# Finer array tiles in the start-up, other banks for the second batch's keys, and a re-sorted instruction order in an attention-then-GLU kernel

## The chip, the cores and the metric

The kernel runs on one core of a Trainium2 chip. The time is the device time of that core in microseconds (us); the figure used is the median of the runs shown. Engines are named as the profile names them: PE is the matmul array (PEld its weight loads), DVE, ACT and POOL the three elementwise engines, SP the engine whose queue issues nearly all DMA transfers.

## The reference

A linear attention with second-order features, and a gated MLP on its output (4 batches, 4 heads, 1088 tokens, head size 32, 8+8 projections):

```python
def phi(x):
    a = np.einsum('rd,bhsd->bhsr', S1, x)
    b = np.einsum('rd,bhsd->bhsr', S2, x)
    return np.einsum('bhsi,bhsj->bhsij', a, b).reshape(*x.shape[:-1], r * r)
q_p, k_p = phi(q), phi(k)
kv = np.einsum('bhsf,bhsd->bhfd', k_p, v);  z = np.sum(k_p, axis=2)
out = einsum(q_p, kv) / (einsum(q_p, z) + 1e-06)          # per head
x = out as [4352 tokens, 128]
xn = x / sqrt(mean(x*x) + 1e-06) * rms_g
y = (silu(xn @ w_gate) * (xn @ w_val)) @ w_out            # d_ff = 1536
```

The weights arrive as 64-bit words and are turned into 32-bit floats on the chip.

## The kernel before

Tokens are cut into nine chunks c0 to c8 (eight of 512 columns, one of 256), and d_ff into twelve slices j. One pair of chunk and slice is a slot: three matmuls into `g_ps` (gate), three into `v_ps` (value), Silu on ACT to `s`, the product `h` on DVE, and the down projection into `o_ps`. Gate and value always take three passes (`x_hi`·`w_hi`, `x_hi`·`w_lo`, `x_lo`·`w_hi`). The down projection is one fp32 matmul (`o_ps<-h,w_f`) in the first twelve slots and the last ones; in all others `h` is split into `h_hi` (a cast, mostly ACT) and `h_lo` (a subtraction, on DVE or POOL) and three passes follow. Slots run c0 with j 0-5, c1 with j 0-5, c0 with j 6-11, c1 with j 6-11, then c2 to c8 whole.

Ahead of a chunk's slots stands its attention. For each batch the keys `kt` go through PE with the small projection `s_t` (lines 489), ACT brings half of the result to `ab`, an outer product makes the features `phi`, and PE sums `phi` against the values `vt` into kv. Batch 0 does this with `o_ps` as accumulator (lines 541); batches 1 to 3 take another form with 32 columns of the array per head (lines 410 to 440). Queries of c0 and c1 go the same way, in token order: A and B by PE (line 582), `abq` on ACT, the outer product `phn` on DVE, a transpose on PE (601), a copy `phiq`. From c2 on, A and B are made transposed (685), copied to `abt`, sent to DRAM (`far`) and read back spread over rows as `at` and `bt`, whose product is `phiq` (line 651, one instruction for each of two halves p0 and p1, on POOL or DVE). Then come the numerator and denominator (669), division, the root (POOL, `rstd`), the scaling `xn`, a transpose (772) and `x_hi`/`x_lo`.

Each weight slice takes an Abs (`w_tmp<-w_raw`, ACT or DVE), four DVE steps (318, 323, 328, 332; the last gives `w_f`), a cast `w_hi` on ACT and a subtraction `w_lo` on POOL.

The order is not that of the code. Every step is put into a `Plan` with a key (its urgency, in slots), a guessed duration on each engine that may do it, and sometimes a penalty for one of them. `Plan.run` places them one by one on guessed clocks and then writes the instructions out in order of guessed start. On the chip each engine works through its own list strictly in that order, so an instruction that waits holds up all that stand behind it in its list. In a wait early in the program the planner has PE do dummy matmuls (line 300).

[...]

Of the kernel before, what the change touches and what calls it, by code (L numbers as in the profile page):

```python
# [21 lines left out]
F = R * R  # L22
NT = B * S
P = 128
# [3 lines left out]
KT = 9  # L28
SP = KT * P
HALF = 64  # L30
# [28 lines left out]
HOP = 160  # L59
COPY_DVE = 600  # L60
REST_DVE = 500
ABS_ACT = -300
NATURAL = 2
PHIS = 2
PUT_DVE = 100
PHIQ_DVE = 600
CUT = 6
TURNED = (1, 2, 3)
HBUFS = 3
# [1 line left out]
EXACT = 2  # L71
EARLY = 12
SPLIT = 6
HEAD = 2
K1 = -41,9,10,-28.2
VT1 = (-15, -14, -13)
SBD = (1,)
AB2 = (-21, -20, -19)
KVO = ()
Q0 = (-61, -57, -56)  # L80
LATER = 12
KLATE = 2500
DLAT = 2400
CHAIN = -52
WAIT = 150
WKEY = {0: -50, 1: -43}
XN_ACT = 150
Q0L = -97.8
Q1 = (8, 6, 5)
Q1L = -25  # L90
KO = (20, 18, 16)
QO = (20, 10, 6)


# [116 lines left out]
def attention_then_glu(ctx, tc, kT, v, qT, sw, w, gain, out):  # L211
    nc = tc.nc
# [9 lines left out]
    def ps(name, bufs):  # L222
        return plan.buf(psum, [P, 512], F32, name, bufs)

    def pe(ns, key, emit, reads, writes, part=False):
        plan.add({"pe": (ns, emit, 0, part)}, key, reads, writes)
# [52 lines left out]
    for b in range(B):  # L279
        t = const.tile([P, 2, 2 * (D + 1)], F32, name=f"kv{b}")  # L280
# [6 lines left out]
    sblk_t = const.tile([P, NB], F32, name="s_t")  # L287
# [110 lines left out]
    abs_of, ahead = {}, {}  # L398
# [65 lines left out]
    def kside(b, keys, early):  # L464
        first = b == 0
        kab, kphi, key = keys
        kt, vt, kv = sb("kt", [P, SP], 2), sb("vt", [P, KT, H, VA], 2), kvs[b]
# [11 lines left out]
        piece = [next(g for g, (_, e) in enumerate(pieces) if hi <= e) for _, hi in groups]  # L479
        abs_ = [sb("ab", [P, 2, 3, H, R], 3) for _ in groups]  # L480
        phis = [sb("phi", [P, 3, H * F], 4) for _ in groups]
# [20 lines left out]
        for i, (lo, hi) in enumerate(groups):  # L502
            g, m, ts = piece[i], hi - lo, slice(0, hi - lo)
            ab_ps, o = (banks[i], 0) if first else (banks[i // 2], i % 2 * 3 * HALF)
            ab, phi = abs_[i], phis[i]
# [28 lines left out]
        acc = ps("o_ps", 1) if first or b in KVO else ps("att", 3)  # L534
        for i, (lo, hi) in enumerate(groups):
            def kvmm(lo=lo, hi=hi, phi=phis[i]):
                kvv = acc()[:, :2 * VA].rearrange("p (a x) -> p a x", x=VA)
                for t in range(lo, hi):
                    for h in range(H):
                        rows = slice((h % 2) * F, (h % 2 + 1) * F)  # L540
                        nc.tensor.matmul(
                            out=kvv[rows, h // 2, :], lhsT=phi()[:, t - lo, h * F:(h + 1) * F], rhs=vt()[:, t, h, :],
                            start=(t == 0 and h < 2), stop=(t == KT - 1), skip_group_check=True,
                        )

            pe(275 * (hi - lo), key, kvmm, [(phis[i], i), (vt, piece[i])], [acc], True)
        for hh in range(2):
            def put(eng, rows=slice(hh * F, (hh + 1) * F), xs=slice(hh * (D + 1), (hh + 1) * (D + 1))):
                kvv = acc()[:, :2 * VA].rearrange("p (a x) -> p a x", x=VA)
# [15 lines left out]
    def qphi(c, kab):  # L565
        n = CHUNKS[c]
        nt = n // P
        first = c == 0
        key0 = kab
        q, phi = phiqs[c]  # L570
        if c < NATURAL:

            ab, pn = sb("abq", [P, 4, H, R], 1), sb("phn", [P, 4, H * F], 1)
            for u in range(0, nt, 2):
                kab = key0 + (1 if first and u else 0)
                us = slice(u, u + 2)
                ab_ps = ps("att", 3)
                tr = ps(("g_ps", "v_ps")[u // 2], 2) if first else ps("att", 3)

                def abmm(u=u, ab_ps=ab_ps):  # L580
                    for t in range(2):
                        nc.tensor.matmul(
                            out=ab_ps()[:, t * HALF:(t + 1) * HALF], lhsT=q()[:, (u + t) * P:(u + t + 1) * P], rhs=sblk_t,
                            start=True, stop=True,
                        )

                def near(ab_ps=ab_ps):
                    return ab_ps()[:, :2 * HALF].rearrange("p (th c r) -> p th c r", c=2, r=R)

                def outer(us=us, near=near):  # L590
                    nc.vector.tensor_tensor(
                        out=pn()[:, us].rearrange("p t (h i j) -> p (t h) i j", h=H, i=R),
                        in0=near()[:, :, 0, :].unsqueeze(3).to_broadcast([P, 2 * H, R, R]),
                        in1=ab()[:, us].rearrange("p t h r -> p (t h) r").unsqueeze(2).to_broadcast([P, 2 * H, R, R]),
                        op=ALU.mult,
                    )

                def turn(u=u, tr=tr):
                    for p in range(2):
                        for t in range(2):  # L600
                            nc.tensor.transpose(
                                out=tr()[:, (2 * p + t) * P:(2 * p + t + 1) * P], in_=pn()[:, u + t, p * P:(p + 1) * P], identity=ident
                            )

                pe(440, kab, abmm, [q, "sblk"], [ab_ps])
                act(
                    HALF, kab, lambda us=us, near=near: nc.scalar.copy(
                        out=ab()[:, us].rearrange("p t h r -> p (t h) r"), in_=near()[:, :, 1, :]
                    ), [ab_ps], [(ab, u)],
                )  # L610
                dve(2 * 268, kab, outer, [(ab, u), ab_ps], [(pn, u)])
                pe(440, kab, turn, [(pn, u)], [tr])

                def put(eng, u=u, tr=tr):
                    eng(out=phi()[:, :, u * P:(u + 2) * P], in_=tr().rearrange("p (a s) -> p a s", a=2))

                plan.add({
                    "act": (512 * 0.835 + 144, lambda put=put: put(nc.scalar.copy), 0),
                    "dve": (512 * 1.04 + 140, lambda put=put: put(nc.vector.tensor_copy), PUT_DVE),
                }, kab, [tr], [(phi, u)])  # L620
        else:


            m = n // 2
            ab, at, bt = sb("abt", [P, 256], 2), sb("at", [P, 2, 512], 1), sb("bt", [P, 2, 512], 1)
            ab_ps = abs_of[c]
            act(m, kab, lambda: nc.scalar.copy(out=ab()[:, :m], in_=ab_ps()[:, :m]), [ab_ps], [ab])
            far = plan.buf(dram, [2 * H * R, 512], F32, "far", 2)
            for t in range(2):
                load(  # L630
                    H * R * n * 4, kab, lambda t=t: nc.sync.dma_start(
                        out=far()[:, t * m:(t + 1) * m], in_=ab()[t * HALF:(t + 1) * HALF, :m]
                    ), [(far, t)], [ab],
                )
            for p in range(2):
                rows = slice(2 * p * R, 2 * (p + 1) * R)
                load(
                    P * n * 8, kab, lambda p=p, rows=rows: nc.sync.dma_start(
                        out=at()[:, p, :n], in_=far()[rows, :n].unsqueeze(1).to_broadcast([2 * R, R, n])
                    ), [(at, p)], [(far, 0), (far, 1)],  # L640
                )
                for o in range(2):
                    rows = slice((H + 2 * p + o) * R, (H + 2 * p + o + 1) * R)
                    load(
                        F * n * 8, kab, lambda p=p, o=o, rows=rows: nc.sync.dma_start(  # L645
                            out=bt()[o * F:(o + 1) * F, p, :n], in_=far()[rows, :n].unsqueeze(0).to_broadcast([R, R, n])
                        ), [(bt, p, o)], [(far, 0), (far, 1)],
                    )

                def times(eng, p=p):  # L650
                    eng.tensor_tensor(out=phi()[:, p, :n], in0=at()[:, p, :n], in1=bt()[:, p, :n], op=ALU.mult)  # L651

                plan.add({
                    "pool": (n * 2.1 + 150, lambda times=times: times(nc.gpsimd), 0),
                    "dve": (n * 1.04 + 140, lambda times=times: times(nc.vector), PHIQ_DVE, True),
                }, kab, [(at, p), (bt, p, 0), (bt, p, 1)], [(phi, "p", p)])
# [35 lines left out]
    def qside(c, keys, also=None):  # L692
        n, s0 = CHUNKS[c], STARTS[c]
        nt = n // P
        first = c == 0
        phi = phiqs[c][1]
        x, xn = sb("x", [P, 4, DM], 2), sb("xn", [P, 4, DM], 1)
# [14 lines left out]
        for u in range(0, nt, 2):  # L712
# [17 lines left out]
            if first and not u:  # L730
                for t in range(2):
# [3 lines left out]
                            out=sq()[:, t], in0=x()[:, u + t], in1=x()[:, u + t], scale=1.0 / DM, scalar=EPS,  # L735
# [4 lines left out]
            if c < ACCUM:  # L740
                for t in range(2):
# [3 lines left out]
                            out=sq()[:, t], in_=x()[:, u + t], func=AF.Square, accum_out=ss()[:, u + t:u + t + 1]  # L745
# [9 lines left out]
        for u, wd in ((0, 2), (2, 2)) if first else ((0, nt),):  # L755
# [2 lines left out]
            xt = ps("att", 3)  # L758
            if first and not u:

                ahead[1] = [ps("att", 3) for _ in range(2)]
            ids = list(range(u, u + wd, 2))

            def root(us=us):
# [14 lines left out]
            if u or not first:  # L779
                dve(  # L780
                    5, kturn, lambda us=us: nc.vector.tensor_scalar(  # L781
                        out=ms()[:, us], in0=ss()[:, us], scalar1=1.0 / DM, scalar2=EPS, op0=ALU.mult, op1=ALU.add
# [130 lines left out]
    for t, (c, j) in enumerate(slots):  # L913
        slot(c, j, t)
        if j == (CUT - 1 if c == 0 else NJ - 1):
            if c + 2 < len(CHUNKS):
                t2 = begin[c + 2]
                if c == 0:
                    qload(2, AB2[0])
                    job = abmm(2)  # L920
# [60 lines left out]
```

## Time and profile before

| | |
|---|---|
| median of 3 runs | 266.39 us (266.28 to 266.45) |
| the profiled execution: its time / its span | 267.68 us / 265.9 us |
| PE busy, DVE, ACT, POOL | 260.0, 189.6, 153.0, 66.8 us |
| granted PE clock | 1.000 |
| DMA, mean over the span | 83 GB/s |

The span runs from the first to the last instruction; the time also holds what lies around them. In the rows, `x24` counts records: an fp32 matmul leaves two, so 36 matmuls are 72 records. The duration of a matmul record contains some 0.2 us of latency; the pace of a row of them is read from start to start.

### The profile page before, as it was taken

The numbers are of one execution on the slowest core, as the hardware profiler recorded it, in microseconds if no ns is written. First come the engines' busy times: TensorE is split into PE (matmuls) and PEld (weight loads), VectorE is DVE, ScalarE is ACT, GpSimd is POOL, SyncE is SP. The second block draws the span as 40 slices with busy tenths as digits, with TensorE's granted clock in tenths as the row PEclk, the third lists the DMA queues.
The fourth block names the chain that finished last, engine by engine and source line by source line (L and its number), as shares of the span: only waits on it lengthen the run. The fifth ranks groups of instructions, "written<-read, shape, count | busy, mean of one in ns | idle before, by whom it ended". The sixth has DMA issues, their size and how long they took to land.

```text
span 265.9 us, 5111 instructions
## 1 busy us (share of the span) xinstructions
PE 260.0 (98%) x1913; PEld 206.8 (78%) x1913; DVE 189.6 (71%) x375; ACT 153.0 (58%) x319; POOL 66.8 (25%) x83
## 2 busy tenths in 40 slices
PE   8989999999989999999999999999999999999995
PEld 6877676678867887878887877788878888788894
DVE  3789997787956886677566796677667566766532
ACT  4377673484744644565556554665656565665662
POOL 5053661265060150002700220012200700100262
PEclk9999999999999999999999999999999999999999
DMA  6999801721511430035002500034002100100010
GB/s 201 362 382 313 264 2 32 218 64 62 148 49 53 125 85 2 1 101 145 13 2 79 140 20 4 0 101 118 1 0 76 55 0 0 42 1 0 0 42 21
DMA packets 13097, 22.11 MB, mean 83 GB/s; under 512 B 1680, under 2 KB 5904, under 8 KB 13072
## 3 DMA queue, kind: packets, MB, share of 16 engines
q1 hardware_dynamic: 12928, 21.72, 26.4%
q8 instruction: 15, 0.25, 0.4%
q14 instruction: 10, 0.08, 0.1%
q10 hardware_dynamic: 144, 0.07, 0.1%
HBM read 18.69 MB, written 3.08 MB: 82 GB/s over the span
## 4 chain that ended last, share of the span: by engine, by line
PE 84%; DMA 8%; SPq 3%; POOL 1%; ACT 1%; issue 1%; DVE 1%; POOLq 0%
PE g_ps L830 25%; PE v_ps L830 25%; PE o_ps L861 21%; DMA w_raw<-w 4%; PE o_ps L848 4%; PE att L669 3%; DMA bt<-far 2%; DMA far<-abt 2%; PE att L414 1%; PE att L685 1%; PE att L772 1%; PE att L489 1%; SPq L645 1%; POOL h_lo L250 1%; POOL phiq L651 0%
## 5 line engine op out<-in xcount | busy, mean ns | idle before, releaser
L841 DVE TENSOR_TENSOR h<-v_ps,s 128x512 f32<-128x512 f32 (+2 forms) x109 | 71.1, 655 | 25.1 <-PE v_ps L830 13.7
L243 ACT CAST h_hi<-h 128x512 fp32r<-128x512 f32 (+1 forms) x91 | 54.2, 596 | 49.2 <-DVE h L841 49.0
L837 ACT ACTIVATE s<-g_ps 128x512 f32<-128x512 f32 (+1 forms) x108 | 62.1, 575 | 25.1 <-PE g_ps L830 22.5
L251 DVE TENSOR_TENSOR h_lo<-h,h_hi 128x512 fp32r<-128x512 f32 x76 | 53.3, 704 | 32.2 <-ACT h_hi L243 31.1
L830 PE MATMUL g_ps<-x_hi,w_hi 128*128 128x512 f32 (+1 forms) x110 | 45.8, 416 | 0.0
L830 PE MATMUL v_ps<-x_hi,w_hi 128*128 128x512 f32 (+1 forms) x110 | 42.0, 382 | 0.0
L830 PE MATMUL g_ps<-x_hi,w_lo 128*128 128x512 f32 (+1 forms) x110 | 41.9, 381 | 0.0
L830 PE MATMUL v_ps<-x_hi,w_lo 128*128 128x512 f32 (+1 forms) x110 | 41.6, 378 | 0.0
L830 PE MATMUL v_ps<-x_lo,w_hi 128*128 128x512 f32 (+1 forms) x110 | 41.5, 378 | 0.0
L830 PE MATMUL g_ps<-x_lo,w_hi 128*128 128x512 f32 (+1 forms) x110 | 41.5, 378 | 0.0
L861 PE MATMUL o_ps<-h_lo,w_hi 128*128 128x512 f32 (+1 forms) x94 | 36.0, 383 | 0.9 <-POOL h_lo L250 0.9
L765 POOL TENSOR_TENSOR rstd<-ms,mhalf 128x4 f32<-128x4 f32 (+1 forms) x10 | 9.2, 924 | 108.8 <-DVE ms L781 108.3
L861 PE MATMUL o_ps<-h_hi,w_lo 128*128 128x512 f32 (+1 forms) x94 | 36.1, 384 | 0.0
L861 PE MATMUL o_ps<-h_hi,w_hi 128*128 128x512 f32 (+1 forms) x94 | 35.9, 382 | 0.0
L830 PEld LDWEIGHTS g_ps<-x_hi,w_hi 128*128 128x128 f32 x110 | 20.7, 188 | 6.3 <-issue 1.5
L651 POOL TENSOR_TENSOR phiq<-at,bt 128x512 f32<-128x512 f32 (+1 forms) x14 | 18.0, 1285 | 29.3 <-DMA bt<-far 22.1
L250 POOL TENSOR_TENSOR h_lo<-h,h_hi 128x256 fp32r<-128x256 f32 (+1 forms) x18 | 18.2, 1018 | 27.4 <-ACT h_hi L243 27.3
L830 PEld LDWEIGHTS v_ps<-x_hi,w_hi 128*128 128x128 f32 x110 | 20.7, 188 | 4.8 <-DVE h L841 0.5
L830 PEld LDWEIGHTS g_ps<-x_hi,w_lo 128*128 128x128 f32 x110 | 20.7, 188 | 4.8 <-issue 1.2
L250 POOL TENSOR_TENSOR w_lo<-w_f,w_hi 128x256 fp32r<-128x256 f32 (+1 forms) x24 | 17.8, 755 | 26.3 <-ACT w_hi L243 26.2
L830 PEld LDWEIGHTS g_ps<-x_lo,w_hi 128*128 128x128 f32 x110 | 20.8, 189 | 4.2
L830 PEld LDWEIGHTS v_ps<-x_lo,w_hi 128*128 128x128 f32 x110 | 20.7, 188 | 4.1
(107 smaller groups left out, 302.7 us busy)
## 6 DMA issues: line engine op xcount, KB each, us to landing
w_raw<-w SPq DMA_DIRECT2D x12, 384.0 KB
at<-far SPq DMA_DIRECT2D x12, 256.0 KB
bt<-far SPq DMA_DIRECT2D x24, 128.0 KB
q<-qT SPq DMA_DIRECT2D x8, 256.0 KB
outT<-o_sb SPq DMA_DIRECT2D x8, 256.0 KB
vt<-v SPq DMA_DIRECT2D x9, 204.0 KB
kt<-kT SPq DMA_DIRECT2D x9, 192.0 KB
far<-abt SPq DMA_DIRECT2D x12, 64.0 KB
```

The lines of the kernel that those rows point to most:

```text
L243: "act": (n * 0.835 + 172, lambda: nc.scalar.copy(out=out(), in_=in_()), 0),
L250: "pool": (n * 2.1 + 150, lambda: nc.gpsimd.tensor_tensor(out=out(), in0=in_(), in1=hi(), op=ALU.subtract), 0),
L251: "dve": (n * 1.04 + 140, lambda: nc.vector.tensor_tensor(out=out(), in0=in_(), in1=hi(), op=ALU.subtract), penalty, True),
L414: nc.tensor.matmul(out=acc()[rows, :F], lhsT=vt()[:, t, h, :D], rhs=phis[t // 3]()[:, t % 3, h * F:(h + 1) * F], start=(t == 0), stop=(t = ...
L651: eng.tensor_tensor(out=phi()[:, p, :n], in0=at()[:, p, :n], in1=bt()[:, p, :n], op=ALU.mult)
L669: nc.tensor.matmul(out=nv[hf * HALF:(hf + 1) * HALF, t, p, :], lhsT=phiqs[c][1]()[:, p, l0:l0 + HALF], rhs=kvs[(STARTS[c] + l0) // S][:, p ...
L765: nc.gpsimd.tensor_tensor(out=rstd()[:, us, 0], in0=ms()[:, us], in1=mhalf[:, us], op=ALU.pow)
L830: nc.tensor.matmul(out=acc()[:, cs], lhsT=wt[:, j, i3, :], rhs=x()[:, cs], start=(i == 0), stop=(i == 2))
L837: act(n, t + 0.3, lambda: nc.scalar.activation(out=s()[:, :n], in_=gps()[:, :n], func=AF.Silu), cols(gps, whole[0]), [s])
L841: lambda cs=cs: nc.vector.tensor_tensor(out=h()[:, cs], in0=vps()[:, cs], in1=s()[:, cs], op=ALU.mult),
L848: lambda cs=cs: nc.tensor.matmul(out=o_ps()[:, cs], lhsT=w_f[:, j, 2], rhs=h()[:, cs], start=first, stop=last and cs.stop == n),
L861: nc.tensor.matmul(out=o_ps()[:, :n], lhsT=wt[:, j, 2, :], rhs=x()[:, :n], start=first and i == 0, stop=last and i == 2,)
```

## The change

Nine things, of which the first three are structure and the others numbers that sort the plan:

- Batch 0's kv: each matmul of 64 output rows becomes two of 32 rows, so a quarter of the array's columns each; the planner's guess falls from 275 to 130 ns per 128 keys.
- A and B of the queries of c0 and c1: each matmul of 128 rows becomes two of 64.
- The two banks for batch 1's A and B are one `g_ps` and one `v_ps` instead of two `att`.
- `HEAD` 2 to 3: the third slot's gate and value too are done in halves of 256 columns.
- `PHIQ_DVE` 600 to 300: the penalty for the product `phiq` on DVE instead of POOL.
- `ABS_ACT` -300 to -500: the bonus for the Abs on ACT.
- `LATER` 12 to 4: how far behind c0's first half its second half is keyed.
- `AB2`, `Q1L`, `KO`: keys of loads and feature steps of c2, c1 and later batches.
- `WKEY`: slice 1's weight load has no key of its own any more.

```diff
-ABS_ACT = -300
+ABS_ACT = -500
-PHIQ_DVE = 600
+PHIQ_DVE = 300
-HEAD = 2
+HEAD = 3
-AB2 = (-21, -20, -19)
+AB2 = (4, -20, 4)
-LATER = 12
+LATER = 4
-WKEY = {0: -50, 1: -43}
+WKEY = {0: -50}
-Q1L = -25
-KO = (20, 18, 16)
+Q1L = -23
+KO = (22, 19, 16)
...
                     for h in range(H):
-                        rows = slice((h % 2) * F, (h % 2 + 1) * F)
-                        nc.tensor.matmul(
-                            out=kvv[rows, h // 2, :], lhsT=phi()[:, t - lo, h * F:(h + 1) * F], rhs=vt()[:, t, h, :],
-                            start=(t == 0 and h < 2), stop=(t == KT - 1), skip_group_check=True,
-                        )
-
-            pe(275 * (hi - lo), key, kvmm, [(phis[i], i), (vt, piece[i])], [acc], True)
+                        for x in range(0, F, F // 2):
+                            r0 = h % 2 * F + x
+                            nc.tensor.matmul(
+                                out=kvv[r0:r0 + F // 2, h // 2, :], lhsT=phi()[:, t - lo, h * F + x:h * F + x + F // 2],
+                                rhs=vt()[:, t, h, :], start=(t == 0 and h < 2), stop=(t == KT - 1), skip_group_check=True,
+                            )
+
+            pe(130 * (hi - lo), key, kvmm, [(phis[i], i), (vt, piece[i])], [acc], True)
...
                     for t in range(2):
-                        nc.tensor.matmul(
-                            out=ab_ps()[:, t * HALF:(t + 1) * HALF], lhsT=q()[:, (u + t) * P:(u + t + 1) * P], rhs=sblk_t,
-                            start=True, stop=True,
-                        )
+                        for hf in range(2):
+                            s0 = (u + t) * P + hf * HALF
+                            nc.tensor.matmul(
+                                out=ab_ps()[hf * HALF:(hf + 1) * HALF, t * HALF:(t + 1) * HALF], lhsT=q()[:, s0:s0 + HALF],
+                                rhs=sblk_t, start=True, stop=True,
+                            )
...
-                pe(440, kab, abmm, [q, "sblk"], [ab_ps])
+                pe(250, kab, abmm, [q, "sblk"], [ab_ps], True)
...
-                ahead[1] = [ps("att", 3) for _ in range(2)]
+                ahead[1] = [ps(name, 2) for name in ("g_ps", "v_ps")]
```

The lines of the changed kernel lie up to four further down than those of before (541 is 543, 582 is 586, 601 is 605, 651 is 655, 772 is 776, 830 is 834, 841 is 845).

**PE in the start-up.** `KV` work is `o_ps<-vt,phi`; `ident,phn` are the transposes of the queries' features, `kv_83,phiq` the numerators of c0, `const-float32` the dummies. Before:

```order
L582 MATMUL att<-s_t,q 128x64 x4
L541 MATMUL o_ps<-vt,phi 64x34 x24
L601 MATMUL g_ps<-ident,phn 128x128 x4
L541 MATMUL o_ps<-vt,phi 64x34 x12
L601 MATMUL v_ps<-ident,phn 128x128 x4
L669 MATMUL att<-kv_83,phiq 64x66 x16
L300 MATMUL att<-const-float32-0.0 1x128 x11
L772 MATMUL att<-ident,xn 128x128 x2
L489 MATMUL att<-s_t,kt 64x64 x18
L772 MATMUL att<-ident,xn 128x128 x2
L830 MATMUL g_ps<-x_hi,w_hi 128x256
```

The same place in the changed kernel:

```order
L586 MATMUL att<-s_t,q 64x64 x8
L543 MATMUL o_ps<-vt,phi 32x34 x32
L605 MATMUL g_ps<-ident,phn 128x128 x4
L543 MATMUL o_ps<-vt,phi 32x34 x40
L605 MATMUL v_ps<-ident,phn 128x128 x4
L673 MATMUL att<-kv_83,phiq 64x66 x16
L300 MATMUL att<-const-float32-0.0 1x128 x2
L489 MATMUL g_ps<-s_t,kt 64x64 x12
L776 MATMUL att<-ident,xn 128x128 x2
L489 MATMUL v_ps<-s_t,kt 64x64 x6
L300 MATMUL att<-const-float32-0.0 1x128 x3
L834 MATMUL g_ps<-x_hi,w_hi 128x256
```

The kv work is 72 matmuls instead of 36 and splits after four of nine key tiles instead of six; batch 1's A and B stand around the first transpose of `xn`, the second transpose behind the first gate matmuls.

**DVE in the start-up**, from the features of c0's queries to c0's division (`den`). Before:

```order
L511 TENSOR_TENSOR phi<-v_ps,ab 128x768
L591 TENSOR_TENSOR phn<-att,abq 128x512 x2
L615 COPY phiq<-g_ps 128x2x256
L318 TENSOR_SCALAR w_tmp<-w_tmp 128x384
L550 COPY kv_83<-o_ps 64x2x33
L323 TENSOR_SCALAR w_tmp<-w_tmp 128x384
L328 SCALAR_TENSOR_TENSOR w_tmp<-w_raw,w_tmp 128x384
L332 SCALAR_TENSOR_TENSOR w_f<-w_raw,w_tmp 128x384
L727 TENSOR_SCALAR den<-att 128x8
```

In the changed kernel:

```order
L595 TENSOR_TENSOR phn<-att,abq 128x512
L511 TENSOR_TENSOR phi<-v_ps,ab 128x768
L595 TENSOR_TENSOR phn<-att,abq 128x512
L552 COPY kv_83<-o_ps 64x2x33
L318 TENSOR_SCALAR w_tmp<-w_tmp 128x384
L323 TENSOR_SCALAR w_tmp<-w_tmp 128x384
L731 TENSOR_SCALAR den<-att 128x8
```

The copy `phiq<-g_ps` has gone to ACT, and slice 0's last two weight steps (328, 332) now stand behind the first `xn`.

**DVE while c3's features are made**, from c2's `x_lo` on. Before:

```order
L775 SCALAR_TENSOR_TENSOR x_lo<-att,gain_t,x_hi 128x512
L841 TENSOR_TENSOR h<-v_ps,s 128x512
L251 TENSOR_TENSOR h_lo<-h,h_hi 128x512 x2
L841 TENSOR_TENSOR h<-v_ps,s 128x512 x2
L251 TENSOR_TENSOR h_lo<-h,h_hi 128x512
```

In the changed kernel:

```order
L779 SCALAR_TENSOR_TENSOR x_lo<-att,gain_t,x_hi 128x512
L845 TENSOR_TENSOR h<-v_ps,s 128x512
L244 CAST h_hi<-h 128x512
L655 TENSOR_TENSOR phiq<-at,bt 128x512
L251 TENSOR_TENSOR h_lo<-h,h_hi 128x512
L845 TENSOR_TENSOR h<-v_ps,s 128x512 x2
L655 TENSOR_TENSOR phiq<-at,bt 128x512
L251 TENSOR_TENSOR h_lo<-h,h_hi 128x512 x2
```

Both products of c3 have moved from POOL into DVE's list. In all, nine of the fourteen `phiq` products now stand on DVE (both of c2, c3, c6 and c7, one of c4); before, all were on POOL.

## The prediction

> **What bounds it now.** I read the page's busy times, then PE's waits, then stretches of the span.
>
> ```profile
> PE 260.0 (98%) x1913; PEld 206.8 (78%) x1913; DVE 189.6 (71%) x375; ACT 153.0 (58%) x319; POOL 66.8 (25%) x83
> PE o_ps L861 <- POOL h_lo L250: 0.9, 1, 0.9
> 12.60:16.00 3.40, 2.63 (x26) 1.76 (x22) 3.08 (x13) 2.17 (x8) 1.44 (x2) 1.00 1.04 407
> 31.00:43.00 12.00, 12.00 (x46) 7.88 (x44) 11.57 (x20) 6.38 (x15) 6.75 (x9) 1.00 0.13 47
> 33.80 0.70 PE g_ps L830 x3
> 37.99 0.86 PE o_ps L848 x2
> ```
>
> PE is the bound: full in 31 to 43 (PE stands first after the length, DVE third, at 11.57 nearly full too); a group of three passes costs it 0.70, a fp32 down matmul 0.86 (the last two rows, from the chain of waits). It has one wait behind the start, 0.9, for a POOL `h_lo`. Ahead of the first gate matmul PE waits for a chain through all engines, and its busy time there holds dummies. So a gain can come from two places: an earlier first gate matmul, with the PE work behind it unchanged, and that wait. The slots' own matmuls are the same in both kernels (the third slot's halves are twice as many at half the length). This is the chain at the start:
>
> ```profile
> 6.39 1.16 PE L582 MATMUL att<-s_t,q 128*128 128x64 f32 x8
> 7.66 1.28 DVE L591 TENSOR_TENSOR phn<-att,abq 128x512 f32<-128x512 f32 x2
> 7.66 1.67 PE L541 MATMUL o_ps<-vt,phi 128*64 128x34 f32 x48
> 9.27 0.66 PE L601 MATMUL g_ps<-ident,phn 128*128 128x128 f32 x4
> 9.52 0.55 ACT L338 ACTIVATE w_tmp<-w_raw 128x384 f32<-128x384 f32 x1 [1.71 <-DMA w_raw<-w]
> 9.85 0.89 PE L541 MATMUL o_ps<-vt,phi 128*64 128x34 f32 x24
> 10.85 0.21 ACT L550 COPY kv<-o_ps 64x66 f32<-64x66 f32 x1 [0.78 <-PE o_ps L541]
> 11.38 1.32 PE L669 MATMUL att<-kv,phiq 128*64 128x66 f32 x32
> 11.35 0.36 DVE L323 TENSOR_SCALAR w_tmp<-w_tmp 128x384 uint32<-128x384 uint32 x1
> 11.75 0.56 DVE L328 SCALAR_TENSOR_TENSOR w_tmp<-w_raw,w_tmp 128x384 uint32<-128x384 uint32 x1
> 12.34 0.56 DVE L332 SCALAR_TENSOR_TENSOR w_f<-w_raw,w_tmp 128x384 uint32<-128x384 uint32 x1
> 12.93 0.17 DVE L727 TENSOR_SCALAR den<-att 128x8 f32<-128x8 f32 x1
> 14.59 0.71 POOL L765 TENSOR_TENSOR rstd<-ms,mhalf 128x2 f32<-128x2 f32 x1 [0.45 <-DVE den L727]
> 15.47 0.42 DVE L768 TENSOR_TENSOR xn<-x,rstd 128x256 f32<-128x256 f32 x1
> 16.38 1.27 PE L489 MATMUL att<-s_t,kt 128*64 128x64 f32 x36
> 18.11 0.27 PE L830 MATMUL g_ps<-x_hi,w_lo 128*128 128x256 f32 x1
> 19.38 0.29 PE L830 MATMUL g_ps<-x_lo,w_hi 128*128 128x256 f32 x1
> 26.98 0.39 PE L830 MATMUL g_ps<-x_hi,w_hi 128*128 128x512 f32 x1
> 43.29 0.34 PE L410 MATMUL att<-ab 128*32 128x32 f32 x17
> 43.50 1.17 PE L414 MATMUL att<-phi,vt 128*32 128x64 f32 x69
> ```
>
> **The quarter tiles, and the price nobody has measured here.** Half tiles pace at 35 ns a record: (9.27 - 7.66 - 0.09 of change-over) / 48 is 32, 1.27 us for 36 is 35, whether 34 or 64 columns move. Quarter tiles with 34 moving columns don't occur. The nearest rows: 69 records with 64 columns in 1.17 - 0.2 of latency, 14 ns; and with 32 columns 17 records from 43.29 until 43.44 or so (43.50 at most), 9 to 12 ns. With 34 columns I take 10, near the second; the ends are 9 and 14. The kv work is then 144 records in 1.44 us (1.3 to 2.0) against 72 at 35, 2.5 us.
>
> [...]
>
> **The chain, step by step** (times of the trace; second figure at 14 ns). A and B in halves: 16 records at 35 ns instead of 1.03 us of pace, so `abq` comes 0.25 us earlier and `phn` can go ahead of the fourth `phi` on DVE, done at 7.75 instead of 8.3. The kv itself I let start at 7.66 as before (its values may be what it waits for). 64 records: 8.30 (8.56). Transposes 0.59 (9.27 to 9.85): 8.89 (9.15). 80 records: 9.69 (10.27), and 0.16 to ACT's `kv` copy: 9.85 (10.43) instead of 10.85. ACT then does slice 0's Abs, whose weights landed by 9.52: 10.5 (11.1); DVE's two short steps, 318 and 323, some 0.3 each from start to start: 11.15 (11.75). PE meanwhile transposes, 0.59, and does c0's first numerators (16 records at (1.32 - 0.2)/32, 0.55, and 0.2 of latency): 11.1 (11.7). So `den` at 11.2 (11.8) instead of 12.93: 1.7 (1.1) earlier, of which 1.0 is the pair 328 and 332 that no longer stands ahead of it. From `den` to `rstd` it is 2.37 (14.59 + 0.71 - 12.93), and no weight step now lies before `xn`: 13.6 to 14.0 (14.2 to 14.65) instead of 15.47 to 15.89.
>
> What is late next is the weight: 328 and 332 follow `xn`, 1.03, so `w_f` 15.0 (15.7), `w_hi` on ACT behind `x_hi` 15.5 (16.15); POOL's list has the second `rstd` ahead of `w_lo`, and its `ms` comes behind 332: 15.8 (16.5), `w_lo` 16.55 (17.3). The second gate pass starts there instead of 18.11: 1.55 (0.8) earlier. The second half of c0 runs through ACT (two copies, two `xn`, an Abs, a cast, `x_hi`) and DVE (slice 1's four steps, `x_lo`): its third gate pass at 18.4 (19.15) instead of 19.38, 1.0 (0.25) earlier.
>
> From there PE has 10 half groups of 0.35, twice transposes (0.45), A/B (0.28) and numerators (0.55), one fp32 down matmul (0.86) and some eight changes between forms at 0.1 (a first gate matmul after one lasts 0.50, at 61.42 below, against 0.39 at 26.98): 7.7 us, of which 0.35 lies before that third pass. 18.4 (19.15) + 7.4 gives 25.8 (26.5) for the point that before had at 26.98. **First term: -1.2 us** (-0.5 at 14 ns; -1.5 if the first half's lead held all through). DVE, nearly full until 43, loses the copy (0.6) and c1's `xn` (0.73, now on ACT) in that time, so I see no new wait there. Batch 1's A and B (1.27 at the same pace in other banks), c1's halves and the fewer dummies lie in PE's wait or cancel: 0, with 0.2 to either side. `ABS_ACT` costs nothing: all Abs were on ACT.
>
> **The features of c2 to c8.** These rows are c2's (45 to 58), c3's (61 to 79), and one of c4, c6 and c7 each; where POOL had waited for `bt`, the start of its row is the landing:
>
> ```profile
> 45.19 0.50 PE L830 MATMUL g_ps<-x_hi,w_hi 128*128 128x512 f32 x1
> 57.55 1.30 POOL L651 TENSOR_TENSOR phiq<-at,bt 128x512 f32<-128x512 f32 x1 [0.92 <-DMA bt<-far]
> 61.42 0.50 PE L830 MATMUL g_ps<-x_hi,w_hi 128*128 128x512 f32 x1
> 61.97 1.14 SPq L631 DMA_DIRECT2D far<-abt  x2
> 66.92 0.56 SPq L638 DMA_DIRECT2D at<-far  x1
> 73.25 1.29 POOL L651 TENSOR_TENSOR phiq<-at,bt 128x512 f32<-128x512 f32 x1 [6.50 <-PE v_ps L830]
> 75.72 1.30 POOL L651 TENSOR_TENSOR phiq<-at,bt 128x512 f32<-128x512 f32 x1 [1.17 <-DMA bt<-far]
> 76.98 1.74 POOL L250 TENSOR_TENSOR h_lo<-h,h_hi 128x512 fp32r<-128x512 f32 x1
> 78.77 0.51 PE L861 MATMUL o_ps<-h_lo,w_hi 128*128 128x512 f32 x1 [0.85 <-POOL h_lo L250]
> 96.15 1.29 POOL L651 TENSOR_TENSOR phiq<-at,bt 128x512 f32<-128x512 f32 x1 [5.46 <-DMA bt<-far]
> 100.34 0.26 PE L414 MATMUL att<-phi,vt 128*32 128x64 f32 x3
> 152.25 1.28 POOL L651 TENSOR_TENSOR phiq<-at,bt 128x512 f32<-128x512 f32 x1 [3.52 <-DMA bt<-far]
> 183.20 1.30 POOL L651 TENSOR_TENSOR phiq<-at,bt 128x512 f32<-128x512 f32 x1 [3.71 <-DMA bt<-far]
> L251 DVE TENSOR_TENSOR h_lo<-h,h_hi 128x512 fp32r<-128x512 f32 x76 | 53.3, 704 | 32.2 <-ACT h_hi L243 31.1
> ```
>
> The wait at 78.77 is a chain: late `bt`, POOL's p1 until 77.0, then the `h_lo`. With both products on DVE it goes: **-0.85 us**. But DVE now stands in its list until the data land, with `h` and `h_lo` behind it. Count from the end of c3's A/B matmuls (61.4). Data of p0 land at +11.8, of p1 at +14.3. In the new order PE's slots (0.70 a group of three) put v21 at +8.25, the 21st down group at +12.45 to +13.15, v24 at +13.85. DVE reaches p0 at about +9.5, waits 2.3, is done at +12.5; `h_lo` 0.6 (0.70 long, started every 0.6): +13.1, needed by the third pass at +12.9: a wait of 0.2. `h` of slot 22 at +13.7, needed (its bank) at +13.85. p1 costs no wait, having landed. The others by the same count: c2's p1 lands 12.35 after its A/B (57.55 - 45.19), its product ends at +13.0, and PE needs it behind seven slots and five down groups at +14.4: 1.4 of slack, of which DVE's own queue may take a part. c4's p0 lands at 96.15; behind it stand `x_lo`, 0.7, not needed for six slots, and batch 2's three `phi`, 2.7: done at 100.1 against 100.34, where PE takes them up. c6's and c7's p0 (152.25, 183.20) land where DVE before stood idle for the next `x_hi`: 0.1 and 0.3 late, with nothing close behind. **Third term: +0.15**, between 0 and +1.5, the upper end if a landing slips by that much, as c3's does against others (+9.3 for c6).
>
> **Sum** against the profiled execution (267.68; its span 265.9): -1.2 - 0.85 + 0.15 = -1.9, so 265.8 and a span of 264.0. The median of the runs is 1.3 below the profiled one; against 266.39 it is **264.5 us**.
>
> **Rivals.**
> - *Only half of the front gain*, by 14 ns a record or by `w_lo` and the second `rstd` meeting on POOL: -0.5 instead of -1.2, 265.2. For it: the second half's lead shrinks to 0.25 there. Against: the 9 to 12 ns of the 32-column row.
> - *DVE takes POOL's place in the wait*: c3's landing as late against DVE as it was against POOL, or c4's phi held up: the 0.85 stays, 265.3. For it: 0.15 to 0.3 us of slack in three places.
> - *A floor under the starts of small matmuls*: quarter tiles pace halfway between the 14 and the 35 ns of the two rows, at 25. Then kv comes at 7.66 + 1.6 + 0.6 + 2.0 + 0.15 = 12.0, 1.15 later than before, `den` at 13.2 in spite of the two steps taken out, and the front term is about 0: 266.39 - 0.85 + 0.15 = 265.7. Against it: the 14 ns themselves, of tiles of the same size. [...]
> - *Nothing moves*: PE's start is set by landings (DMA share 1.04 in 12.6 to 16) and one wait follows the other: 266.4. Against: slice 0's weights were there at 9.52, 3.4 us ahead of their `w_f`.
> - *Slower*: DVE blocked in its list. c3's slack ends at +11.6; each microsecond of later landing is a microsecond of PE, and the gain of 1.9 with the threshold is lost from about +14 for p0 on, or with 1.2 us in c3 and as much in c4: 267.2. For it: POOL's waits for `bt` in the rows above, 3.5 to 5.5 us, which mostly cost PE nothing on POOL. Against: no landing in this trace is later than +11.8.
>
> **Chances.** Forecast 0.47 (its own range 264.1 to 265.0); half 0.14; DVE in POOL's place 0.12; floor 0.07; nothing 0.09; slower 0.11. Faster by over 0.2% (0.53 us, about what a measurement can tell from no change): the first four, 0.80; same 0.09; slower 0.11. The last two lie above 266.0, so the range is 263.9 (front -1.5, no DVE wait, another -0.2) to 266.0.
>
> **What would show it.** Right: `kv` on ACT at 9.9, `den` at 11.2, first `w_lo` pass at 16.6, the first fp32 down matmul done by 25.8; kv records 10 ns apart; no PE wait for POOL; DVE waiting for `bt` some 2 us in c3 with PE waiting at most 0.3. Wrong: kv records at 14 or 25 ns; PE's first slots waiting for `w_lo`; PE waiting for `h` or `h_lo` behind `phiq`.

## The result, and the profile after

The changed kernel takes 269.97 us (269.55 to 270.46, 4 runs) against 266.40 (266.28 to 266.45, 4 runs) for the kernel before on the same chip: 1.0135 times as long, 95% interval 1.0115 to 1.0156. It is slower by 3.6 us where 1.9 less was forecast. Its profiled execution took 270.26 with a span of 268.5.

The page's busy times, then three of PE's four waits (the fourth, 0.8, stands ahead of its first dummy), in the changed kernel:

```profile
PE 259.3 (97%) x1995; PEld 205.1 (76%) x1995; DVE 193.2 (72%) x381; ACT 154.0 (57%) x326; POOL 55.1 (21%) x76
PE att L673 <- issue: 3.5, 1, 3.5
PE att L586 <- DMA q<-qT: 0.8, 1, 0.8
PE g_ps L834 <- DVE x_lo L779: 0.4, 1, 0.4
```

PE's wait for POOL's `h_lo` is gone, as forecast. There is a new one of 3.5 us on `issue`: no semaphore and no other engine that the profile shows ends it. PE's timeline shows its place (start, duration, line, records, the idle time before it):

```profile
7.59 0.76 PE L543 MATMUL o_ps<-vt,phi 128*32 128x34 f32 x64
8.29 0.66 PE L605 MATMUL g_ps<-ident,phn 128*128 128x128 f32 x4
8.88 0.91 PE L543 MATMUL o_ps<-vt,phi 128*32 128x34 f32 x80
9.76 0.66 PE L605 MATMUL v_ps<-ident,phn 128*128 128x128 f32 x4
10.41 0.33 PE L673 MATMUL att<-kv,phiq 128*64 128x66 f32 x2
14.19 1.56 PE L673 MATMUL att<-kv,phiq 128*64 128x66 f32 x30 [3.45 <-issue]
20.24 0.39 PE L834 MATMUL g_ps<-x_hi,w_lo 128*128 128x256 f32 x1
32.83 1.02 PE L852 MATMUL o_ps<-h,w_f 128*128 128x512 f32 x2
```

Up to 10.41 everything runs as forecast: 64 quarter-tile records in 8.29 - 0.09 - 7.59, 9.5 ns each, 80 in 9.76 - 0.09 - 8.88, 10 ns. Then PE does 2 of the 32 records of c0's numerators and stands still in the middle of them. ACT's and DVE's timelines say what hangs on it:

```profile
9.88 0.21 ACT L552 COPY kv<-o_ps 64x66 f32<-64x66 f32 x1 [0.30 <-PE o_ps L543]
14.91 0.17 DVE L731 TENSOR_SCALAR den<-att 128x8 f32<-128x8 f32 x1 [3.58 <-PE att L673]
```

`kv` comes at 9.88 (forecast 9.85), `den` at 14.91 (forecast 11.2). The row at 32.83 is one fp32 down matmul, the second of the fifteen in the kernel; it serves below to compare kernels. By stretches of the span (length; busy time and records of PE, PEld, DVE, ACT, POOL; PE's granted clock; DMA share; GB/s):

```profile
10.52:14.19 3.67, 0.22 (x2) 0.08 (x3) 0.72 (x2) 1.06 (x3) 0.00 (x0) 1.00 1.04 409
14.19:18.06 3.87, 3.87 (x58) 3.06 (x57) 2.90 (x12) 0.69 (x4) 0.71 (x1) 0.56 0.80 314
76.00:100.00 24.00, 24.00 (x170) 19.38 (x169) 19.41 (x37) 12.96 (x25) 2.64 (x3) 1.00 0.31 84
```

In the stop the DMA engines are full (1.04); behind it PE runs at a mean clock of 0.56 until 18.06, where before had 1.00 in the same stretch. In 76 to 100, where before had its wait for POOL, PE is full now.

### The profile page after: what moved, and what is told of

It is laid out like the page before. It is cut to its first block, busy times and chain, and to the rows that moved or that the text cites. A ratio compares the mean times of both kernels' runs of the same rounds, so it can differ in the third digit from the quotient of the medians.

```text
span 268.5 us, 5268 instructions
## 1 busy us (share of the span) xinstructions
PE 259.3 (97%) x1995; PEld 205.1 (76%) x1995; DVE 193.2 (72%) x381; ACT 154.0 (57%) x326; POOL 55.1 (21%) x76
## 4 chain that ended last, share of the span: by engine, by line
PE 91%; DVE 3%; issue 2%; DMA 2%; ACT 1%; SPq 0%; POOL 0%
PE g_ps L834 27%; PE v_ps L834 26%; PE o_ps L865 23%; PE o_ps L852 4%; PE att L673 4%; DMA q<-qT 2%; PE att L776 1%; PE att L414 1%; PE att L689 1%; PE att L489 1%; PE o_ps L543 1%; PE g_ps L489 1%; DVE w_tmp L318 0%; DVE w_f L332 0%; DVE phn L595 0%
## 5 line engine op out<-in xcount | busy, mean ns | idle before, releaser
L243 ACT CAST h_hi<-h 128x512 fp32r<-128x512 f32 (+1 forms) x89 | 52.9, 595 | 48.5 <-DVE h L845 48.4
L251 DVE TENSOR_TENSOR h_lo<-h,h_hi 128x512 fp32r<-128x512 f32 x74 | 51.3, 698 | 33.3 <-ACT h_hi L243 32.4
L834 PE MATMUL g_ps<-x_hi,w_hi 128*128 128x512 f32 (+1 forms) x111 | 46.6, 420 | 0.0
L250 POOL TENSOR_TENSOR h_lo<-h,h_hi 128x512 fp32r<-128x512 f32 (+1 forms) x20 | 20.7, 1040 | 68.5 <-ACT h_hi L243 68.4
L834 PEld LDWEIGHTS v_ps<-x_hi,w_lo 128*128 128x128 f32 x111 | 20.9, 188 | 4.2 <-issue 0.2
L250 POOL TENSOR_TENSOR w_lo<-w_f,w_hi 128x256 fp32r<-128x256 f32 (+1 forms) x24 | 15.4, 656 | 25.2 <-ACT w_hi L243 25.1
```

What stands on the lines that cost most here:

```text
L243: "act": (n * 0.835 + 172, lambda: nc.scalar.copy(out=out(), in_=in_()), 0),
L250: "pool": (n * 2.1 + 150, lambda: nc.gpsimd.tensor_tensor(out=out(), in0=in_(), in1=hi(), op=ALU.subtract), 0),
L251: "dve": (n * 1.04 + 140, lambda: nc.vector.tensor_tensor(out=out(), in0=in_(), in1=hi(), op=ALU.subtract), penalty, True),
L834: nc.tensor.matmul(out=acc()[:, cs], lhsT=wt[:, j, i3, :], rhs=x()[:, cs], start=(i == 0), stop=(i == 2))
```

## The experiments

Four theories. **A**: PE ran out of instructions. Its stream comes in blocks by DMA, and the next block was behind the data loads. **B**: the numerators wait for something that the trace hides (kv, `phiq`, a bank). **C**: the fewer dummies and PE's clock are the cause, the stop only goes with them. **D**, for what was left once A was shown: the lead at `den` is lost later in the start. In the rows an instruction count is matmul plus weight-load records; an fp32 matmul leaves two of each. The diffs here leave out what isn't needed to see the change (`...`). The expectations count batches from 1: what they call batch 1's kv and values are those of batch 0 in the text ahead of the prediction. "The stop" is PE's wait on `issue`.

### Where PE stops

Without the first dummies:

```diff
-WARM = 8
+WARM = 0
```

> The changed kernel without the 8 dummy matmuls (16 records with as many weight loads) with which PE begins; everything else in the same order. Theory A (PE runs out of instructions: the next block of its instruction stream, about 256 instructions, is fetched by DMA behind the data loads and isn't there when the 449th recorded PE instruction is due): the stop moves back by the 32 instructions taken out, into the numerators of c0, after 18 of their 32 records instead of after 2, and still ends between 14.0 and 14.8 us; time 269.3 to 270.5. Theory B (the third numerator record waits for something hidden: kv, phiq, a bank): the stop stays after 2 records. Theory C (no stop of its own, the clock gate and the missing dummies are what costs): no rule for the place, PE's clock at half from the start, 270 or more.

Before, with quarter tiles in kv and nothing else:

```diff
-    out=kvv[rows, h // 2, :], lhsT=phi()[:, t - lo, h * F:(h + 1) * F], ...
+    for x in range(0, F, F // 2): ...   # two matmuls of 32 rows, guess of 275 kept
```

> The kernel before with only batch 1's kv matmuls cut to quarter tiles, its order as it was (144 PE instructions more early on, all 11 dummies behind the numerators kept). Theory A: the stop appears in this kernel too, after some 10 of the 32 numerator records, and ends near 14; den at 14.5 or later instead of 12.93; time 267.3 to 269.5. Theory B or C (the cause lies in the changed order, the banks, or the fewer dummies): no stop, den at 11.5 to 12, time 265.4 to 266.4.

Many small dummies first:

```diff
-    keep_warm(WARM)()
+    for _ in range(50):
+        nc.tensor.matmul(out=warm[:1, :4], lhsT=zeros[:, :1], rhs=zeros[:, :4], start=True, stop=True)
```

> The changed kernel with 50 dummies of 4 columns in place of the 8 of 128 at PE's start: 168 recorded PE instructions MORE ahead of everything else. Theory A: what counts is where the edges of the blocks fall and when each fetch is asked for. The first fetch is then asked for in the dummies, ahead of most loads, and its edge falls in the kv at 8.2 to 8.9 us; the next one falls behind the numerators; the stop of 3.5 us goes or shrinks under 1.2; time 264.2 to 266.5. Theory B: stop as it was, 269.5 to 270.5. Theory C: 269 to 271, since the dummies behind the numerators are as few. That more instructions are simply worse: 271 or more.

Measured: 268.48 (1.0064 times before, 1.0039 to 1.0088), 268.55 (1.0071, 1.0037 to 1.0104) and 268.83 (1.0080, 1.0065 to 1.0095). The stops, from PE's timelines, two rows each in the same order:

```profile
11.05 0.98 PE L673 MATMUL att<-kv,phiq 128*64 128x66 f32 x18
14.25 0.63 PE L673 MATMUL att<-kv,phiq 128*64 128x66 f32 x14 [2.23 <-issue]
10.77 0.56 PE L671 MATMUL att<-kv,phiq 128*64 128x66 f32 x10 [0.16 <-DVE kv L552]
13.70 0.92 PE L671 MATMUL att<-kv,phiq 128*64 128x66 f32 x22 [2.36 <-issue]
13.58 0.56 PE L491 MATMUL g_ps<-s_t,kt 128*64 128x64 f32 x10
15.91 0.62 PE L491 MATMUL g_ps<-s_t,kt 128*64 128x64 f32 x14 [1.77 <-issue]
```

And what PE had done until just before it went on, in the changed kernel, then in the same three (the counts in the first two brackets are the records of PE and PEld):

```profile
0.00:14.15 14.15, 8.90 (x222) 6.13 (x223) 6.27 (x15) 5.64 (x15) 4.02 (x17) 1.00 0.83 293
0.00:14.20 14.20, 7.62 (x222) 6.59 (x223) 7.55 (x22) 5.60 (x15) 4.73 (x18) 1.00 0.81 285
0.00:13.65 13.65, 9.67 (x222) 7.13 (x222) 7.11 (x18) 5.74 (x16) 4.81 (x18) 1.00 0.85 304
0.00:15.85 15.85, 12.32 (x350) 10.66 (x351) 8.54 (x27) 6.26 (x19) 4.80 (x18) 1.00 0.88 317
```

The stop stands at a count, not at a place: after 222 matmuls and 223 (222) weight loads, whether that is 2, 18 or 10 records into the numerators, in the changed order or in the old one. With the four or five semaphore and drain records that these columns leave out, the traces have 449 instructions ahead of it in each of the three. The fourth row stops at 350 and 351, 256 more: there the first edge (the end of a block) passed without a stop and the second one caught PE in other work. B would have left the place as it was, and C has no rule for it; before with its 22 dummy records kept stops too, so the quarter tiles of kv alone are enough. **A is shown.** That 32 instructions fewer at the head moved the stop back by 16 matmuls, and 168 more took it away from there, also says that what counts is where the edges fall.

Not all came as expected. Without first dummies 269.3 to 270.5 was expected and 268.48 measured: PE gets to the stop later (12.0 instead of 10.7) and goes on at about the same time (14.25). In before with quarter tiles `den` is at 14.19, 14.5 or later expected. With small dummies 264.2 to 266.5 was expected: the second edge cost 1.8 us, and behind dummies of 4 columns PE was as slow as without any: four transposes take 1.12 us in both (8.87 and 8.41 in their timelines) against 0.66 at 8.29 above, behind the 8 of 128, though the granted clock of the stretches around them reads 1.00 each time.

Instructions taken out again, kv in halves with the changed order:

```diff
+    out=kvv[rows, h // 2, :], lhsT=phi()[:, t - lo, h * F:(h + 1) * F], ...   # 64 rows again, guess of 130 kept
```

> The changed kernel with batch 1's kv in half tiles as before, its order as changed: 72 matmul records and 72 weight loads fewer ahead of the numerators. Theory A: the 449th instruction comes 144 later, behind the numerators and dummies, so no stop there; kv copied on ACT at about 10.9, den at 12.2 to 12.5; PE's wait for POOL gone; time 265.0 to 266.0. Theory B: the stop of 3.5 us stays behind the second numerator record, 269.5 to 271. Theory C: the dummies are as few as in the changed kernel, so 268.5 or more.

```profile
11.36 1.35 PE L671 MATMUL att<-kv,phiq 128*64 128x66 f32 x32
```

All 32 numerators in one row, no stop, as A has it; `kv` (10.83) and `den` (12.31) come as expected too. But the time is 266.97, 1.0002 (0.9987 to 1.0017) of before: a microsecond above what was expected. The stop is one thing, and the forecast gain missing without it another.

### What the block waits for

The section on DMA queues, for the stretch 11.7 to 12.8 of the changed kernel, has the block (packets, MB, share of 16 engines); from 7.8 to 11.7 there is none:

```profile
q1 hardware_dynamic: 157, 0.43, 98.1%
q8 instruction: 1, 0.02, 5.6%
```

One packet of 0.02 MB, from 11.73 to 12.71 in the trace; PE goes on 1.5 us after its end. The trace of before has the same packet from 11.96 to 12.89, so the block came as late there: but its PE starts the 449th instruction at 17.07 only, and nothing waits.

In what follows, "held loads" is the kernel with one small DMA more that holds SP's queue up, and "first halves" the one with the first piece of kv in half tiles again:

```diff
+            if j == 1:
+                nc.sync.dma_start(out=held, in_=values[0]()[:1, KT - 1, H - 1, :4])
             nc.sync.dma_start(out=raw()..., in_=w...)
```

> The changed kernel with one more small DMA on SP ahead of the weight slices 1 and later: it copies four of batch 1's values, so SP stands until those values have landed (about 8.3 us) and has 0.8 MB less of loads out when PE asks for its next block of instructions (at 7.8 us). Theory A with its cause (the fetch queues behind the loads that are out: 1.36 MB at 0.4 MB/us is 3.4 us, seen 3.9): the block's packet starts at 9.0 to 10.0 instead of 11.7, PE goes on at 11.4 to 12.5 instead of 14.2, the stop after the second numerator record is 0.8 to 1.9 us instead of 3.5, den at 12.1 to 13.2; time 266.3 to 268.5. Rival (a fetch takes about 6.4 us from its asking, whatever the loads): stop of 3.5 as before, 269.5 to 271.

```profile
10.41 0.33 PE L675 MATMUL att<-kv,phiq 128*64 128x66 f32 x2
11.75 1.10 PE L675 MATMUL att<-kv,phiq 128*64 128x66 f32 x30 [1.01 <-issue]
12.41 0.17 DVE L733 TENSOR_SCALAR den<-att 128x8 f32<-128x8 f32 x1 [1.09 <-PE att L675]
```

The packet now runs from 9.42 to 10.34, PE stops at the same record and goes on at 11.75, 2.4 us earlier; `den` at 12.41. The time is 267.63, 1.0033 (1.0018 to 1.0048): 2.7 of the 3.6 us are back with every matmul as in the changed kernel. From 9.3 to 11.2 the loads' queue q1 moves 0.35 MB instead of 0.73. So the block does stand behind the loads that are out; the rival of a fixed 6.4 us falls. Other traces bear this out: with held loads and first halves the packet starts between 9.3 and 9.6 too, without held loads at 11.96 in before and between 11.2 and 11.6 in before with quarter tiles and with kv in halves. The exception is the run with small dummies, where PE is through 222 matmuls at 9.9 without a stop, so the block was there by then; there PE starts its 193rd instruction, 256 ahead of the 449th, at 3.1 us instead of 7.8. (When a block is asked for, the trace doesn't show. The next packet starts at 17.14 in the changed kernel and at 19.62 in before, 2.95 us behind the end of the stop (14.19) and 2.55 behind the start of the 449th instruction (17.07).)

> As the run with held loads, and PE's first 8 dummies of 128 columns made into 2 of 512: the same columns in 24 instructions fewer. Theory A: the stop comes after 14 of the 32 numerator records and ends where it does in the run with held loads, so that less is left to do behind it: 0.1 to 0.3 us faster than that, 266.0 to 268.3. Rival (place fixed): as that run.

```diff
-    keep_warm(WARM)()
+    for _ in range(2):   # 512 columns each, rhs=zeros.unsqueeze(1).to_broadcast([P, 4, P])
```

Its stop comes after 14 numerator records and ends at 11.87, as A says; the 0.1 to 0.3 us that were expected from it are not seen: 267.65 (1.0023, 1.0007 to 1.0039).

> As the run with held loads and 2 wide dummies, and the first piece of batch 1's kv back in half tiles (64 instructions fewer, some 0.5 us longer). Theory A: the 449th instruction now lies behind all 32 numerator records, where PE waits for xn anyway; no stop that counts; kv on ACT at 10.3 to 10.6, den at 11.6 to 12.3 (12.93 before), first down matmul and all behind it ahead of before's; time 265.0 to 266.2. Rival (the start isn't worth anything once the stop is gone, as in the run with all kv in halves): 266.4 to 267.2.

```diff
+                        wx = F // 2 if lo >= HALVES else F   # HALVES = 4
```

> The changed kernel with 2 wide dummies and the first piece of kv in half tiles, loads not held: 88 PE instructions fewer than changed. Theory A: the stop moves behind the numerators, into the work that fills PE's wait for xn; block there at about 14.2, when xn's transposes are due at 14.1, so 0.1 to 0.6 us are lost against the same with held loads (266.4): 266.4 to 267.2. If holding the loads itself costs (weights later), it comes out even or ahead: 266.0 to 266.4. Rival B (place fixed behind the second numerator record): stop of 3 us, 269 or more.

With held loads: no stop, 266.44, 0.9980 (0.9970 to 0.9990), the one version that is faster than both kernels by more than its interval, if by 0.2% alone. That misses A's 265.0 to 266.2 and lies where its rival had it. Without holding: 266.66, 0.9992 (0.9975 to 1.0009), and the stop where A puts it, in the filling work behind the numerators:

```profile
12.30 0.56 PE L494 MATMUL g_ps<-s_t,kt 128*64 128x64 f32 x10
13.53 0.62 PE L494 MATMUL g_ps<-s_t,kt 128*64 128x64 f32 x14 [0.66 <-issue]
```

### Where the rest of the forecast went

With held loads and first halves `den` comes where the forecast had it, partly by luck: kv starts at 6.86 here instead of the 7.66 of the forecast, and its first piece in halves takes longer. DVE, POOL twice, then PE, from its timelines:

```profile
11.26 0.17 DVE L739 TENSOR_SCALAR den<-att 128x8 f32<-128x8 f32 x1
15.14 0.70 POOL L777 TENSOR_TENSOR rstd<-ms,mhalf 128x2 f32<-128x2 f32 x1 [1.68 <-DVE ms L793]
15.81 0.94 POOL L251 TENSOR_TENSOR w_lo<-w_f,w_hi 128x256 fp32r<-128x256 f32 x1
16.80 0.39 PE L842 MATMUL g_ps<-x_hi,w_lo 128*128 128x256 f32 x1 [0.76 <-POOL w_lo L251]
18.61 0.39 PE L842 MATMUL g_ps<-x_lo,w_hi 128*128 128x256 f32 x1
28.79 1.02 PE L860 MATMUL o_ps<-h,w_f 128*128 128x512 f32 x2
```

The last row is the second of the fifteen fp32 down matmuls (its two records are the 28th and 27th last), which can be matched between kernels by counting from the end.

> The kernel before, unchanged, as one of the kernels timed, so that this chip's execution of it leaves a trace. If PE's wait for POOL's h_lo near 78 us (0.85 in the trace of before) belongs to the program, it is there again and the span is 265 to 266; if it depends on when the data land, it may be 0 to 0.85, with the span 264.3 to 265.2 where it is absent. Ratio 1.000 within 0.002.

Ratio 1.0020 (0.9991 to 1.0049). Four of PE's waits there, and the same down matmul, behind it that of before's first trace:

```profile
PE att L772 <- DVE xn L768: 0.8, 1, 0.8
PE att L300 <- PEq L974: 0.8, 1, 0.8
PE g_ps L489 <- DMA kt<-kT: 0.4, 1, 0.4
PE o_ps L848 <- DVE h L841: 0.2, 1, 0.2
28.56 1.02 PE L848 MATMUL o_ps<-h,w_f 128*128 128x512 f32 x2
29.08 1.02 PE L848 MATMUL o_ps<-h,w_f 128*128 128x512 f32 x2
```

No wait for POOL in this execution (266.18, span 264.4), though POOL does the same work: it starts c3's second product at 74.67 instead of 75.72, and its `h_lo` behind that takes 1.32 instead of 1.74. The one on which the forecast rests (267.68) had that wait, 0.85, and this matmul at 29.08, 0.52 later: together 1.4 of its excess of 1.5. So two executions of one kernel differ by half a microsecond at this point, and smaller differences between single traces show nothing by themselves.

> The kernel before with only PHIQ_DVE at 300 (both products of a chunk's query features go to DVE or POOL as the changed kernel has them). Prediction's second and third terms: PE's wait of 0.85 for POOL's h_lo goes and DVE's waits cost 0.15: ratio to before 0.9965 to 0.998. Rival (DVE takes POOL's place in the wait, or that wait comes and goes with the landings): 0.999 to 1.002. A start that changes as well would show in den later than 13.1.

```diff
-PHIQ_DVE = 600
+PHIQ_DVE = 300
```

266.62, 0.9989 (0.9977 to 1.0001), outside the 0.9965 to 0.998 expected and at the edge of the rival's range: the two terms that were to bring 0.70 bring 0.3 at the median, if anything. Its second down matmul stands at 28.81, so the start with held loads and first halves (28.79) shows no lead at this point, though its second gate pass leads by 1.06 (16.80 against 17.86).

> The kernel before with PHIQ_DVE at 300 and quarter tiles only for the kv matmuls of the key tiles from 4 on (80 PE instructions more ahead of the numerators, all dummies kept, no order changed). Theory A: the 449th instruction then lies in the dummies behind the numerators, where PE waits for xn anyway, so a stop there costs nothing; kv on ACT 0.4 to 0.6 earlier than in the run with PHIQ_DVE alone (10.6), den at 12.1 to 12.3 instead of 12.67, xn 0.3 to 0.5 earlier, and with all weights' steps ahead of it as before, PE's first slots by as much: ratio to before 0.996 to 0.998, 265.8 to 266.4. Rival (the lead at den is lost on the way to the gate, as with held loads): ratio as with PHIQ_DVE alone, 0.999.

The start of before with 40 matmul records more, stopped in the dummies as expected:

```profile
11.79 1.27 PE L301 MATMUL att<-const-float32-0.0 128*1 128x128 f32 x10
13.55 1.49 PE L301 MATMUL att<-const-float32-0.0 128*1 128x128 f32 x12 [0.49 <-issue]
```

`kv` (10.01) and `den` (12.21) come as expected, but the time doesn't: 266.44, 0.9987 (0.9971 to 1.0002), as the rival has it. The second down matmul is at 28.34, 0.5 ahead of the run with `PHIQ_DVE` alone in the traces, and the times don't tell the two apart.

> As the run with held loads, wide dummies and the first kv piece in halves (no stop; den at 11.3, but the second gate pass only at 16.8 since POOL's second rstd stands ahead of the first slice's w_lo), with that one w_lo on DVE; the second half's xn goes to DVE with it. Theory D (the start's lead of 1.2 us at den is lost where w_lo and the second rstd meet on POOL): second gate pass at 15.9 to 16.2, PE's wait of 0.76 for w_lo under 0.3, second xn transposes 0.3 to 0.7 earlier than 17.15; ratio to before 0.995 to 0.9975, 265.4 to 266.1. Rival (DVE's list is as full: slice 1's w_f comes later by 0.8, and the second slot waits for it): ratio 0.998 to 1.001, as without it.

```diff
+    rest(..., -3000 if j == 0 and xs.start == 0 else REST_DVE)   # was REST_DVE
```

```profile
PE o_ps L551 <- DMA vt<-v: 1.0, 2, 0.8
PE att L594 <- DMA q<-qT: 0.7, 1, 0.7
PE att L613 <- DVE phn L603: 0.3, 1, 0.3
```

The wait for `w_lo` is gone (the pass 4.7 us behind `den` instead of 5.5), and PE waits for c1's queries instead, whose load stands behind the weights. 266.94, 1.0005 (0.9990 to 1.0021), in the rival's range, and the second gate pass is at 16.48 instead of the 15.9 to 16.2 expected, in an execution whose `den` was 0.5 later (11.80) because the values landed later. Half of D holds: the wait for `w_lo` took part of the lead, but freeing it hands the wait to the loads. How much of this is the holding of the loads itself was not tried, nor were the other numbers of the plan (`HEAD`, `LATER`, `AB2`, `Q1L`, `KO`, `WKEY`, `ABS_ACT`) one by one.

## Why the prediction was wrong, point by point

- **The step that failed** stands in the chain: "PE meanwhile transposes, 0.59, and does c0's first numerators", done at 11.1, and so `den` at 11.2. PE did reach the numerators (10.41), but stood still after 2 of their 32 records until 14.19, and `den` came at 14.91. The sum had prices for what PE's instructions take to run (1.44 us for kv) and none for bringing them. Ahead of the numerators the changed kernel has 80 matmul records more (72 of kv, 8 of A and B), with as many weight loads: PE is through its first 449 instructions at 10.7, where before starts the 449th at 17.07, and the next block could be used at 14.2 only. This is the whole change of sign: the second down matmul is at 32.83 in the changed kernel and at 28.79 where the first piece of kv is in halves, the first dummies are fewer and the loads are held, 4.0 us. 3.45 is the stop; the clock of 0.56 behind it is part of the rest. The fewer dummies behind the numerators, which the forecast put at 0, are not the cause: before with all of them kept stops too.
- **Quarter tiles**: right. 9.5 and 10 ns a record (forecast 10). The 25 ns of the rival with a floor, halfway between the paces of two rows, don't show; `kv` comes at 9.88.
- **The chain from `den` to `w_lo`**: near the mark where PE isn't stopped, `den` at 11.26 (11.2), `w_lo` finished at 16.75 (16.55), but in a kernel with an earlier start of kv and a slower first piece, so that `den` agrees partly by luck.
- **From there to -1.2**: wrong. The third pass of the second half comes at 18.61 (18.4), but the forecast took it as a point with the same work behind it. From there to the sixth of the fifteen fp32 down matmuls (37.53) PE takes 18.92 us and 120 records; with `PHIQ_DVE` alone it takes 18.43 us (19.13 to 37.56) and 110 records. The changed order has 0.5 us more left at that point, which is the lead that it had. At the second down matmul the term is 0.0 against that run, +0.2 against before's second trace and -0.3 against its first: all far from -1.2, and too close to 0 to give a sign.
- **PE's wait for POOL**: the wait is gone and none of PE's takes its place, as forecast, but its worth was wrong, and so was the reading of c3. DVE was to wait 2.3 us there for data landing 11.8 behind A/B; in the changed kernel it starts that product 9.6 behind A/B (76.17) without a wait. The row at 73.25, taken for the landing, names PE's `v_ps` as what ended the wait and not the DMA. DVE's 2.2 us of waits for `bt` stand in later chunks (1.40 at 155.63, 0.82 at 185.83), so that the "some 2 us" of the forecast agree by luck. As to the worth: from the second down matmul to `xn`'s transposes for a later chunk (93.38 in before's first trace, 95.96 changed) the changed kernel's lag falls from 3.75 to 2.58, 1.2 us; against before's second trace (91.91) it falls from 4.27 to 4.05, 0.2 us.
- **The base**: the terms were read on an execution 1.3 above the median, and then taken from the median. As far as two traces of before show it, the wait and the late start were in those 1.3, so they were counted twice. Held loads and first halves took 266.16 when profiled, 1.5 less than 267.68 (the forecast -1.9), and 0.02 less than before's second trace.
- The rivals had the right sign in one case (DVE blocked in its list), by a mechanism that doesn't appear: no wait of PE stands behind DVE's.

Of the 5.5 us of error, 4.0 go to the stop and its clock, which the runs show. The other 1.5 (-1.9 forecast, 266.44 against 266.88 measured without the stop) go to the front term, the wait for POOL and the base; how they share it is read from single traces.

## What to carry to other kernels

Count PE's instructions, not only their time, wherever a change cuts matmuls finer early in a kernel: a stop in the middle of equal matmuls that the profile puts down to `issue`, at the same count whatever is run (here 449 recorded ones, or 256 more), points to a missing block of instructions. Here fewer instructions, fewer and wider dummies, or fewer loads out at that time moved it. Before a wait is counted as a gain, ask whether the executions near the median have it. A lead at one step is worth what is left at a point with the same work behind it, best matched by counting matmuls of one kind from the end.

## What the runs showed of the hardware

- PE's instructions come in packets of 0.02 MB on a queue of their own (q8; 15 packets, 0.25 MB in the traces of before and of the changed kernel), with edges 256 recorded instructions apart (222 + 223 and 350 + 351). From the packet's end until PE went on it took 1.5 us in the changed kernel (12.71 to 14.19) and 1.4 with held loads (10.34 to 11.75). In the changed kernel's stop the DMA engines were at 1.04. In these runs PE stopped after 449 recorded instructions, or 256 more behind the small dummies, for 0.5 to 3.5 us; in before, which starts the 449th at 17.07, 4.2 us behind the packet's end (12.89), it didn't stop there.
- After the stop PE's clock stood at half from 14.64 to 18.06 (0.50), though PE was at work again from 14.19; that execution's mean clock was 0.994. In the profiled executions with stops of 2.2 and 2.4 us the mean clock was 0.998 and 1.000. In the one with the stop of 1.8 behind the small dummies it was 0.993, and there gate passes of 256 columns start 0.21 us apart at 18.88 and 0.12 from 21.05 on, so the length of the stop alone doesn't decide. Executions of one kernel differ too: of the ten of before with quarter tiles, five with a mean clock of 0.987 to 0.994 took 269.11 to 270.75 us, and five with 0.999 to 1.000 took 266.88 to 267.99. Only one of the second five has a trace.
